# A gated mix of dilated local attention and a 2-D spectral filter: weight blocks prepared once for both parities, odd positions prepared early, folds in other buffers, odd unfolds on GpSimd

## The chip, the cores and the metric

The kernel runs on one core of one Trainium2 chip. The metric is the device time of one execution in microseconds (us). The core has five engines with queues of their own: TensorE (PE, matmuls, with its weight loads shown as PEld), VectorE (DVE), ScalarE (ACT), GpSimd (POOL) and SyncE (SP, which here only issues DMA transfers). A queue is in order: an instruction that waits holds up everything behind it on the same engine.

## The reference, cut to what matters

```python
S, D = 2048, 640                              # positions, channels; everything float32
def _A_ref(x, wqkv, wo):                      # local attention, 32 heads of 20
    W, dil = 8, 2
    qkv = x @ wqkv                            # 640 x 1920, split into q, k, v
    idx = pos[:, None] - (arange(W) * dil)    # a position looks at itself and 7 earlier ones, 2 apart
    logits = where(idx >= 0, einsum("bhsd,bhswd->bhsw", q, k[idx]) * 20 ** -0.5, -1e9)
    o = einsum("bhsw,bhswd->bhsd", softmax(logits), v[idx])
    return o @ wo
def _B_ref(x, w_r, w_i):                      # spectral filter
    return irfft2(rfft2(x) * (w_r + 1j * w_i))
g = sigmoid((x * gate_w).sum(-1, keepdims=True))
return g * _A_ref(x, wqkv, wo) + (1 - g) * _B_ref(x, w_r, w_i)
```

Because the window steps by 2, even positions look only at even ones and odd positions only at odd ones. The two parities are independent in attention.

## The kernel before, in words

**Layout.** A partition holds 16 consecutive positions, j = 0 to 15, so `x` is 128 partitions x 16 positions x 640 channels. Even j belong to parity 0, odd j to parity 1.

**Projection (`load_x`, `load_w`, `qkv`).** TensorE multiplies fp32 numbers as fp32r in three products: each operand is split into a rounded high part (a cast on ScalarE) and a low part (a subtraction on VectorE or GpSimd), and hi x hi, hi x lo and lo x hi are summed. The weights come as four head groups hg = 0 to 3 of five blocks each (128 x 480). For one parity and one hg, `qkv` runs eight positions of fifteen products, copies each result out of PSUM on ScalarE (`ev`) and stores it to DRAM (`qkvd`). Seven PSUM banks (`BP`) rotate among these. Even x (`xe`) and hg 0 are read into the buffers `x0` to `x6` first; odd x (`xo`) comes later, in `x0` to `x7`. Before, all four head groups are run for the even positions (0, 1, 2, 3), then for the odd ones (3, 2, 1, 0). Three of the four weight groups are loaded and split a second time for the odd ones. A split of hg 1 is on VectorE, seven times from a copy in PSUM (`ws`); the other loaded ones are on GpSimd.

**Folds (`fold`, `load_f`, `cols`).** For the transform along the channels, `fold` adds and subtracts mirrored halves of x for two positions at once (q = 0 to 7; six two-input operations on SBUF data, all on VectorE). Folds 0 and 1 stay in SBUF; the other six are stored to DRAM by GpSimd's queue and read back. `cols` multiplies a folded pair by a transform over the partitions (`z`), and ScalarE copies the result into `zg`, which lies where the even x lay. So no `cols` can begin before the last even projection.

**Attention (`attend`).** Sixteen units (parity, h), two per head group. A unit loads k, q, v from DRAM, VectorE multiplies q (copied into the PSUM bank `qbank` by ScalarE) with shifted k (`pr`) and sums over the head's 20 channels (`L`); softmax follows; GpSimd multiplies with v (`pv`) and VectorE sums (`o`), which goes to DRAM (`od`). Some units give the last of their four `pr` to GpSimd. Before, the units are the eight even ones, then the odd ones h = 6, 7, 4, 5, 2, 3 and, interleaved, 0 and 1.

**Spectral stage (`freq`).** Sixteen groups of frequencies in the order 1, 2, 3, 0, 4 to 15. For each: products `u`, `v` over the channels, sum and difference (`ab`), a transform (`xa`, and for the other half `xc`), multiplication by the filter, the transform back (`g`). The filter needs each half also turned by 90 degrees. Groups 0 to 3 get this by a second product (`xb`, `xd`); groups 4 to 15 (`TURN`) by two half-height copies on ScalarE.

**The end (`spatial`, `project_even`, `project_odd`).** `spatial` transforms back over channels and partitions (`oa`, `ob`, `ha`, `hb`). Even rows are unfolded on VectorE (`h`, `ha`, `y`) and added on GpSimd to the projected attention, which was stored before (`yi`). For odd rows the halves are kept (`ho`), and `project_odd` unfolds them in five operations (`ye`, `y`), transposes the attention output (`oTp`, `oT`), multiplies it by `wo` (`woa`, `wob`, 30 products) and adds it to `y`. Four buffers for `y` serve even and then odd rows.

**The order of the work** is planned ahead: a model of the engines (`Plan.cost`, with `LATE` for latencies and `RATE` and `QUEUE` for transfers) gives each instruction a start, and each engine gets its instructions in that order. A hundred random variations are tried on the model. Dependences through buffers are kept, in the order in which the functions are called: a buffer's next owner waits for every access of the owner before. The model lets a VectorE operation with two SBUF inputs wait for GpSimd (`two`, `WAIT`).

All planned instructions have the same line in the profile, 638, so they are told apart by their tiles' names. The lines of the program that the change touches are: the earliest start of loads (297), the planner's constants (476 to 479), the rings of buffers (549 to 556), the order of calls (`work`, 570), `load_w` (656), `load_x` (681), `qkv` (706), `fold` (825), and the tables `WPLACES`, `ODD_POOL`, `FOLD_DVE`, `TURN` (1132 to 1147).

Of the kernel before, what the change touches and what calls it, by code (L numbers as in the profile page):

```python
# [13 lines left out]
F32 = mybir.dt.float32  # L14
# [141 lines left out]
class Plan:  # L156
# [121 lines left out]
    def order(self):  # L278
        ops = self.ops
        for op in ops:  # L280
            op.lat += LATE.get(op.chain, 0.0) * (not op.size or op.chain in ("swap", "f"))
        for op in ops:
            for p in op.preds:
                p.succs.append(op)
        last = {}
        for op in reversed(ops):
            op.tail = max([s.tail + self.lag(op, s) for s in op.succs], default=0.0)
            if op.size:
                op.tail += op.size / RATE
            key = (op.eng, op.chain)  # L290
            if key in last and (op.eng == "PE" or op.chain and op.eng != "ACT"):
                op.tail = max(op.tail, last[key].tail)
            op.tail += op.busy
            last[key] = op
        span = max(op.tail for op in ops)
        for op in ops:
            op.early = max(0.0, span - op.tail - AHEAD) if op.early else 0.0
            op.tail += BIAS.get(op.chain, 0.0)
        rng = np.random.default_rng(SEED)
        self.draws = [rng.exponential(size=len(ops)).tolist() for _ in range(DRAWS)]  # L300
        best = self.turns(TURNS)

        names = {n: i for i, n in enumerate(dict.fromkeys(op.of for op in ops))}
        family = np.array([names[op.of] for op in ops])
        for _ in range(AGAIN):
            move = MOVE * rng.choice([0.3, 1.0, 2.0]) * rng.normal(size=len(names))
            move *= rng.random(len(names)) < rng.choice([0.1, 0.5, 1.0])
            for op, t in zip(ops, (best[1] + move[family]).tolist()):
                op.tail = t
            best = min(best, self.turns(2), key=lambda b: b[0])  # L310
        self.ends = best[0], best[3]
        order = []
        for op, op.start, op.end in best[2]:
            order.append(op)
        return order
# [157 lines left out]
DRAWS, SOONEST, LATER_BY = 3, 2.4, 0.6  # L473
ENGS = ("PE", "DVE", "ACT", "POOL", "SP")
RATE = 380e3
QUEUE = 250e3
LAND = 3.2
LATE = {"w": 1.0, "f": 4.0, "x": 3.5, "swap": 1.5}
AHEAD = 130.0
WAIT = 1.3  # L480
PACE = 1.02
EDGE = {("POOL", "ACT"): 2.0, ("DVE", "ACT"): 1.0}
# [4 lines left out]
def staged(gens, n):  # L487
    for step in range(len(gens) + n - 1):
        for i in range(max(0, step - n + 1), min(step, len(gens) - 1) + 1):
            next(gens[i], None)  # L490
# [14 lines left out]
class Mixer:  # L505
# [17 lines left out]
    def places(self, pp, dr, sb):  # L523
        self.pp, self.sb = pp, sb
        qb = self.pp.tile([128, 512], F32, tag="qbank", name="qbank")
        self.qthird = [qb[:, GC * i : GC * i + GC] for i in range(3)]
        self.qturn = -1
        self.qkv_d = dr.tile([8, 6, ROWS, HC], F32, tag="dram_qkv", name="qkvd")
        self.o_d = [dr.tile([128, 8, D], F32, tag=f"dram_o{i}", name=f"od{i}") for i in range(2)]
        self.f_d = dr.tile([128, 8, 2, D], F32, tag="dram_f", name="fd")  # L530
        self.a_d = dr.tile([128, 8, D], F32, tag="dram_a", name="ad")
        self.ident, self.fc = (self.one(n, 128) for n in ("ident", "fc"))
        self.fct = self.one("fct", 2, 128)
        self.z, self.g, self.ng, self.nng = (self.one(n, NJ) for n in ("z", "g", "ng", "nng"))
        make_identity(self.nc, self.ident)
        self.low = self.one("low", 64)
        self.nc.gpsimd.memset(self.low, -1e9)

        def ring(*tags):
            return Ring(sb, *tags)  # L540

        def n(tag, k):
            return ring(*(f"{tag}{i}" for i in range(k)))


        self.kvr, self.Lr, self.qr, self.prr = n("kv", 6), n("L", 3), n("q", 2), n("pr", 2)
        self.mr, self.sr, self.orr, self.pvr = n("m", 2), n("s", 2), n("o", 2), n("pv", 2)

        self.xr, self.wr, self.evr, self.rawr, self.fr = n("x", 8), ring(*WPLACES), n("ev", 2), n("raw", 5), n("f", 2)
        self.er = ring("e0", "e1")  # L550

        self.zcr, self.vsr, self.mdr, self.mfr, self.wpr = n("raw", 2), ring("raw2"), n("ev", 2), ring("mf"), n("f", 2)
        self.abr, self.Pr, self.s12r, self.Xr = ring("x0", "x1"), ring("x2", "x3"), ring("x4", "x5"), ring("raw3", "raw4")
        self.p1r = ring("x6")

        self.wor, self.war, self.yar = ring("ya", "w7"), n("w", 7), ring("ya")
        self.otr, self.oTr = (ring("w7"), ring("w7", "kv2")), (ring("x7"), ring("x7", "pr0"))
        self.osr, self.hor, self.hyr, self.yer = n("raw", 3), n("x", 4), ring("x4", "x5"), ring("x6")
        self.yr, self.yir = ring("raw3", "raw4", "e0", "ya"), n("f", 2)
        self.banks = {}  # L560
# [9 lines left out]
    def work(self):  # L570
# [12 lines left out]
        S.dma_start(self.fc, ins["t_fc"][:, 0:128])  # L583
        self.zero_rows()
        self.qkv(0, 0)
        self.load_w(None, 1)
        for q in range(8):
            self.fold(q)
        self.qkv(0, 1)
        self.load_w(None, 2)  # L590
        self.qkv(0, 2)
        self.load_w(None, 3)
        for j in range(1, NJ, 2):
            self.load_x(None, self.xr.next(f"xo{j}", 2, 5, 128, dtype=F32R), j)
        self.qkv(0, 3)
        self.zg = self.one("zg", 5, NJ, 128, tag="big")
        for hg in (3, 2, 1, 0):
            self.qkv(1, hg)
            if hg:
                self.load_w(None, hg - 1)  # L600
                for q in {3: (0, 1), 2: (2, 3), 1: (4, 5, 6, 7)}[hg]:
                    self.cols(q)
                    if q < 6:
                        self.load_f(q + 2)
        self.bt, self.gt = self.one("bt", 1288, tag="e0"), self.one("gt", 1288, tag="e1")
        S.dma_start(self.bt[:, 0:1284], ins["t_bt"])
        S.dma_start(self.gt, ins["t_gt"])
        S.dma_start(self.fct.rearrange("p v m -> p (v m)"), ins["t_fc"][:, 128:384])
        self.gates()
        self.load_wo()  # L610
        for h in range(8):
            staged([self.attend(0, h)], 3)
        for h in (6, 7, 4, 5, 2, 3):
            staged([self.attend(1, h)], 3)
        pair = [self.attend(1, h, 2) for h in (0, 1)]
        for _ in range(5):
            for a in pair:
                next(a, None)
# [23 lines left out]

    def zero_rows(self):
        p, d = self.p, self.qkv_d
        zero = self.one("zero", 7 * HC, tag="pv0")[0:32]
        p.pool.memset(zero, 0.0)
        p.pool.dma_start(
            bass.AP(
                tensor=d.tensor,
                offset=d.offset + 2 * ROWS * HC,  # L650
                ap=[[6 * ROWS * HC, 8], [ROWS * HC, 4], [1, 7 * HC]],
            ),
            zero,
        )

    def load_w(self, st, hg):
# [4 lines left out]
        for t in range(5):  # L661
# [5 lines left out]
                p.sp.dma_start(raw, src[t])  # L667
            p.chain = "w" if st is None else ""
            p.act.copy(hi[t], raw)
            if hg == 1 and (t > 2 or 1 in self.xT) or (hg, t, 1 in self.xT) in W_DVE:  # L670
                b = self.ps(BP, f"ws{t}")[:, 0:n]
                p.act.copy(b, raw)
                raw = b
            (p.pool if hg != 1 and st is None and (hg, t, 1 in self.xT) not in W_DVE else p.dve).tensor_sub(lo[t], raw, hi[t].bitcast(F32))
            p.chain = ""

    def load_chunk(self, place, hg, t):
# [3 lines left out]
    def load_x(self, st, pair, j):  # L681
        p = self.p
        hi, lo = self.xT[j] = [pair[:, i].rearrange("p t a -> p (t a)") for i in range(2)]
        raw = (self.rawr.next(f"xt{j}", 640) if st is None else st.pop(0))[:, 0:640]
        self.xraw[j] = raw
        src = self.ins["xT"][j].rearrange("p t a -> p (t a)")
        p.chain = "" if j else "first"
# [15 lines left out]
            (p.pool if st is None else p.dve).tensor_sub(lo, raw, hi.bitcast(F32))  # L703
        p.chain = ""

    def qkv(self, par, hg):
        p, d = self.p, self.qkv_d
        n = 482 if hg == 0 else 480
        u = 4 * par + hg
        for jj in range(8):  # L710
# [17 lines left out]
            if jj % 2:  # L728
# [3 lines left out]
                    ap=[[8 * HC, 128], [ROWS * HC, 6], [1, 2 * HC]],  # L732
                )
                p.act.dma_start(to, ev.rearrange("p i j c -> p i (j c)"))

    def gates(self):
        p = self.p
# [87 lines left out]
    def fold(self, q):  # L825
        p = self.p
        G = p.dve if q in FOLD_DVE else p.pool
        xt = (self.fr if q < 2 else self.xr).next(f"fx{q}", 2, 641)
        p.sp.dma_start(xt, self.ins["x"][:, 2 * q : 2 * q + 2, :])
        e = self.er.next(f"fe{q}", 2, 321)  # L830
        f, o = xt[:, :, 0:640], xt[:, :, 0:321]
        rv = xt[:, :, 640:319:-1]
# [3 lines left out]
        G.tensor_add(f[:, :, 480:640], o[:, :, 1:161], o[:, :, 319:159:-1])  # L836
        G.tensor_add(f[:, :, 0:161], e[:, :, 0:161], e[:, :, 320:159:-1])
        G.tensor_sub(f[:, :, 161:321], e[:, :, 0:160], e[:, :, 320:160:-1])
        if q < 2:
            self.folded[q] = f  # L840
        else:
            p.pool.dma_start(self.f_d[:, q], f)

    def load_f(self, q):
        f = self.folded[q] = self.fr.next(f"f{q}", 2, 641)[:, :, 0:640]
# [283 lines left out]


WA, WB, WC = ("w0", "w1", "w2", "w3", "w4"), ("w5", "w6", "w7", "w0", "w1"), ("w2", "w3", "w4", "e0", "e1")
WPLACES = WA + WB + WC + WB + WC + WB + ("w2", "w3", "w4", "e1", "w5")

WHOLE = tuple((0, t) for t in range(5))
ODD_POOL = ()
XO_DVE = ()
W_DVE = ()
FOLD_DVE = tuple(range(8))

# [2 lines left out]
POOL_PR = {u: (6,) for u in ((0, 3), (0, 4), (0, 5), (0, 7), (1, 0), (1, 1), (1, 3), (1, 4), (1, 5), (1, 7))}  # L1144


TURN = tuple(range(4, 16))


def build(tc, ins, out):  # L1150
# [45 lines left out]
```

## Time and profile before

| | |
|---|---|
| median of 3 runs | 465.52 us (464.35 to 465.58) |
| profiled execution, its own time | 463.47 us |
| its span, first to last instruction | 461.7 us |
| mean granted TensorE clock | 0.996 |
| busy: PE, PEld, DVE, ACT, POOL | 449.5, 393.3, 422.1, 219.4, 319.5 us |
| DMA traffic | 105.90 MB, mean 229 GB/s |
| weight block loads (`raw`) | 25 of 240 KB and 5 of 241 KB |

An engine's busy time is the union of its instructions, and overlapping matmuls are counted once. In a row of groups, "x15 | 25.0, 1560 | 10.5 <-ACT X 10.5" means: fifteen instructions, 25.0 us busy together, 1560 ns one, and 10.5 us in which the engine stood idle before them, released by ScalarE's `X`. A fp32 product shows as two records ("x2").

### The profile page before, as it was taken

The numbers are of one execution on the slowest core, as the hardware profiler recorded it, in microseconds if no ns is written. First come the engines' busy times: TensorE is split into PE (matmuls) and PEld (weight loads), VectorE is DVE, ScalarE is ACT, GpSimd is POOL, SyncE is SP. The second block draws the span as 40 slices with busy tenths as digits, with TensorE's granted clock in tenths as the row PEclk, the third lists the DMA queues.
The fourth block names the chain that finished last, engine by engine and source line by source line (L and its number), as shares of the span: only waits on it lengthen the run. The fifth ranks groups of instructions, "written<-read, shape, count | busy, mean of one in ns | idle before, by whom it ended". The sixth has DMA issues, their size and how long they took to land.

```text
span 461.7 us, 7202 instructions
## 1 busy us (share of the span) xinstructions
PE 449.5 (97%) x2449; PEld 393.3 (85%) x2449; DVE 422.1 (91%) x555; ACT 219.4 (48%) x575; POOL 319.5 (69%) x264
## 2 busy tenths in 40 slices
PE   8899999999999999999999999999999999998997
PEld 4688888888889889899887878879988999987996
DVE  3599979999998999899999999899999999999594
ACT  4432455524326354254457477777665454341110
POOL 1001656999999869879898988477587996964200
PEclk9999999999999999999999999999999999998999
DMA  8999999786777988868887776657643321365832
GB/s 309 395 392 297 371 386 310 260 275 196 249 248 199 324 250 263 267 173 298 294 282 238 216 226 213 236 158 249 192 150 92 89 88 51 128 194 138 267 124 85
DMA packets 71700, 105.90 MB, mean 229 GB/s; under 512 B 20704, under 2 KB 50400, under 8 KB 71664
## 3 DMA queue, kind: packets, MB, share of 16 engines
q1 hardware_dynamic: 40624, 69.90, 46.6%
q10 hardware_dynamic: 30128, 31.55, 21.5%
q0 software_dynamic: 912, 4.00, 2.2%
q8 instruction: 19, 0.31, 0.3%
q14 instruction: 17, 0.14, 0.1%
HBM read 72.59 MB, written 32.84 MB: 228 GB/s over the span
## 4 chain that ended last, share of the span: by engine, by line
PE 83%; DVE 9%; DMA 4%; ACT 2%; issue 2%; SPq 0%; ACTq 0%; DVEq 0%
PE qkv L638 43%; PE woa L638 7%; PE wob L638 6%; PE z L638 4%; PE oa L638 3%; PE ob L638 3%; PE g L638 3%; PE u L638 2%; PE v L638 2%; PE oTp L638 2%; PE xc L638 2%; DMA raw<-in_wqkv 2%; DMA st<-in_xT 1%; PE hb L638 1%; PE ha L638 1%
## 5 line engine op out<-in xcount | busy, mean ns | idle before, releaser
L638 PE MATMUL qkv<-w,xo 128*128 128x480 f32 (+1 forms) x480 | 109.7, 384 | 0.0
L638 PE MATMUL qkv<-w,xe 128*128 128x480 f32 (+1 forms) x465 | 103.4, 382 | 2.1 <-ACT xe L638 1.5
L638 PEld LDWEIGHTS qkv<-w,xe 128*128 128x128 f32 x465 | 87.3, 188 | 18.0 <-ACT xe L638 3.0
L638 PEld LDWEIGHTS qkv<-w,xo 128*128 128x128 f32 x480 | 89.8, 189 | 13.5
L638 ACT COPY ev<-qkv 128x480 f32<-128x480 f32 x64 | 35.3, 559 | 74.5 <-PE qkv L638 69.3
L638 PE MATMUL woa<-wo,oT 128*128 128x320 f32 x240 | 50.6, 321 | 0.0
L638 PE MATMUL wob<-wo,oT 128*128 128x320 f32 x240 | 50.0, 318 | 0.6 <-ACT oT L638 0.6
L638 PEld LDWEIGHTS woa<-wo,oT 128*128 128x128 f32 x240 | 39.4, 192 | 0.5
L638 PEld LDWEIGHTS wob<-wo,oT 128*128 128x128 f32 x240 | 39.0, 190 | 0.9 <-ACT oT L638 0.8
L638 POOL DMA_DIRECT2D fd<-fx x6 | 4.3, 722 | 42.4 <-DVE fx L638 42.4
L638 POOL TENSOR_TENSOR P<-X,wp 128x642 f32<-128x642 f32 x16 | 25.0, 1560 | 10.5 <-ACT X L638 10.5
L638 POOL TENSOR_TENSOR w<-raw,w 128x480 fp32r<-128x480 f32 (+1 forms) x20 | 25.3, 1278 | 8.0 <-ACT w L638 5.3
L638 ACT CAST oT<-oTp 128x384 fp32r<-128x384 f32 (+1 forms) x32 | 13.3, 427 | 31.8 <-PE oTp L638 22.7
L638 PEld LDWEIGHTS g<-mm,s 128*128 128x128 f32 x150 | 22.5, 190 | 6.4 <-ACT zg L638 1.7
L638 PE MATMUL g<-mm,s 128*128 128x128 f32 x150 | 24.9, 278 | 1.4 <-DVE s L638 0.7
L638 PE MATMUL u<-bt,zc 128*128 128x321 f32 (+2 forms) x96 | 23.3, 344 | 0.0
L638 PE MATMUL ob<-gt,zg 128*128 128x161 f32 (+1 forms) x96 | 23.1, 344 | 0.0
L638 PE MATMUL v<-bt,zc 128*128 128x321 f32 (+2 forms) x96 | 22.9, 344 | 0.0
L638 POOL TENSOR_TENSOR yi<-yi,y 128x640 f32<-128x640 f32 x8 | 12.6, 1569 | 14.2 <-DMA yi<-ad 11.4
L638 PE MATMUL oa<-gt,zg 128*128 128x161 f32 (+1 forms) x96 | 22.0, 344 | 0.0
L638 ACT CAST w<-raw 128x480 fp32r<-128x480 f32 (+1 forms) x30 | 17.4, 594 | 7.1 <-PE qkv L638 5.3
L638 DVE TENSOR_TENSOR oT<-oTp,oT 128x384 fp32r<-128x384 f32 (+1 forms) x32 | 15.2, 482 | 3.7 <-ACT oT L638 3.7
(304 smaller groups left out, 1113.6 us busy)
## 6 DMA issues: line engine op xcount, KB each, us to landing
qkvd<-ev ACTq DMA_DIRECT2D x32, 480.0 KB, 4.3
wp<-in_ws SPq DMA_DIRECT2D x16, 642.0 KB, 4.3
raw<-in_wqkv SPq DMA_DIRECT2D x25, 240.0 KB, 6.7
fx<-in_x SPq DMA_DIRECT2D x8, 641.0 KB, 9.0
ot<-od SPq DMA_DIRECT2D x16, 320.0 KB, 3.4
fd<-fx POOLq DMA_DIRECT2D x6, 640.0 KB, 6.0
f<-fd SPq DMA_DIRECT2D x6, 640.0 KB, 5.7
xt<-in_xT SPq DMA_DIRECT2D x8, 320.0 KB, 4.9
```

Source lines behind the costliest of these rows:

```text
L638: p.dve.memset(w, 0.0)
```

## The change

- Each weight group is loaded and split once. The order of projections becomes (even, 0), (odd, 0), (even, 1), (odd, 1), (even, 2), (even, 3), (odd, 2), (odd, 3). Loaded blocks are all split on GpSimd; the copies through PSUM are gone.
- The odd positions are loaded and split right after the even ones, from raw buffers of their own (`xor`).
- The folds use the buffers `pr0`, `pr1`, `pv0`, `pv1`, `f0`, `f1`; folds 6 and 7 stay in SBUF, fold 7 is made by GpSimd, the stores are issued by ScalarE's queue, and the loads have an earliest start in the plan. The zeros for the rows before the first position move from `pv0` to `ya`.
- `cols` are called between the positions of the last two projections, 6 and 7 first.
- The attention units take the order of `UNITS`.
- Odd rows are unfolded on GpSimd.
- Groups 1, 2 and 3 are turned by copies as well.
- The planner's constants for a queue's rate and for the odd positions' lateness change. The raw `wo` blocks keep their buffers, the split ones get others.

```diff
-            op.early = max(0.0, span - op.tail - AHEAD) if op.early else 0.0
+            op.early = max(FOLD * (op.chain == "fold"), span - op.tail - AHEAD) if op.early else 0.0
...
-QUEUE = 250e3
+QUEUE = 330e3
-LATE = {"w": 1.0, "f": 4.0, "x": 3.5, "swap": 1.5}
+LATE = {"w": 1.0, "f": 4.0, "x": 1.0, "swap": 1.5}
+FOLD = 14.0
...
-        self.er = ring("e0", "e1")
+        self.er, self.xor = ring("e0", "e1"), ring("raw0", "raw1", "raw2", "raw3", "raw4", "kv4", "kv5", "ya")
-        self.wor, self.war, self.yar = ring("ya", "w7"), n("w", 7), ring("ya")
+        self.wor, self.war, self.yar = ring("ya", "w7"), ring("w2", "w3", "w4", "w0", "w1", "w5", "w6"), ring("ya")
...
         self.qkv(0, 0)
-        self.load_w(None, 1)
         for q in range(8):
             self.fold(q)
-        self.qkv(0, 1)
-        self.load_w(None, 2)
-        self.qkv(0, 2)
-        self.load_w(None, 3)
         for j in range(1, NJ, 2):
             self.load_x(None, self.xr.next(f"xo{j}", 2, 5, 128, dtype=F32R), j)
-        self.qkv(0, 3)
+        self.qkv(1, 0)
+        for hg in (1, 2, 3):
+            self.load_w(None, hg)
+            self.qkv(0, hg)
+            if hg == 1:
+                self.qkv(1, hg)
         self.zg = self.one("zg", 5, NJ, 128, tag="big")
-        for hg in (3, 2, 1, 0):
-            self.qkv(1, hg)
-            if hg:
-                self.load_w(None, hg - 1)
-                for q in {3: (0, 1), 2: (2, 3), 1: (4, 5, 6, 7)}[hg]:
-                    self.cols(q)
-                    if q < 6:
-                        self.load_f(q + 2)
+        todo = [6, 7, 0, 1, 2, 3, 4, 5]
+
+        def columns(jj):
+            if jj % 2:
+                self.cols(todo.pop(0))
+                if len(todo) > 1:
+                    self.load_f(todo[1])
+
+        self.qkv(1, 2, columns)
+        self.qkv(1, 3, columns)
...
-        for h in range(8):
-            staged([self.attend(0, h)], 3)
-        for h in (6, 7, 4, 5, 2, 3):
-            staged([self.attend(1, h)], 3)
-        pair = [self.attend(1, h, 2) for h in (0, 1)]
+        for u in UNITS[:-2]:
+            staged([self.attend(*u)], 3)
+        pair = [self.attend(*u, 2) for u in UNITS[-2:]]
...
-            if hg == 1 and (t > 2 or 1 in self.xT) or (hg, t, 1 in self.xT) in W_DVE:
-                b = self.ps(BP, f"ws{t}")[:, 0:n]
-                p.act.copy(b, raw)
-                raw = b
-            (p.pool if hg != 1 and st is None and (hg, t, 1 in self.xT) not in W_DVE else p.dve).tensor_sub(lo[t], raw, hi[t].bitcast(F32))
+            (p.dve if st is not None else p.pool).tensor_sub(lo[t], raw, hi[t].bitcast(F32))
...
-        xt = (self.fr if q < 2 else self.xr).next(f"fx{q}", 2, 641)
+        xt = self.one(f"fx{q}", 2, 641, tag=FOLDS[q])
+        p.chain = "fold"
         p.sp.dma_start(xt, self.ins["x"][:, 2 * q : 2 * q + 2, :])
+        p.chain = ""
...
-        if q < 2:
+        if q > 5:
             self.folded[q] = f
         else:
-            p.pool.dma_start(self.f_d[:, q], f)
+            p.act.dma_start(self.f_d[:, q], f)
...
-WPLACES = WA + WB + WC + WB + WC + WB + ("w2", "w3", "w4", "e1", "w5")
+WPLACES = WA + WB + WC + WB
-ODD_POOL = ()
+ODD_POOL = tuple(range(1, 16, 2))
-FOLD_DVE = tuple(range(8))
+FOLD_DVE = tuple(range(7))
-TURN = tuple(range(4, 16))
+TURN = tuple(range(1, 16))
+UNITS = ((0, 0), (0, 1), (1, 0), (1, 1), (0, 2), (0, 3), (0, 4), (0, 5), (0, 6), (0, 7), (1, 2), (1, 3), (1, 4), (1, 5), (1, 6), (1, 7))
+FOLDS = ("pr0", "pr1", "pv0", "pv1", "f0", "f1", "f0", "f1")
```

More of the change, by code (lines that the diff above doesn't have):

```diff
@@ L644, in zero_rows @@
         p, d = self.p, self.qkv_d
-        zero = self.one("zero", 7 * HC, tag="pv0")[0:32]
+        zero = self.one("zero", 7 * HC, tag="ya")[0:32]
         p.pool.memset(zero, 0.0)
@@ L683, in load_x @@
         hi, lo = self.xT[j] = [pair[:, i].rearrange("p t a -> p (t a)") for i in range(2)]
-        raw = (self.rawr.next(f"xt{j}", 640) if st is None else st.pop(0))[:, 0:640]
+        raw = (self.xor.next(f"xt{j}", 640) if st is None else st.pop(0))[:, 0:640]
         self.xraw[j] = raw
@@ L704, in load_x, with qkv @@
         p.chain = ""
-    def qkv(self, par, hg):
+    def qkv(self, par, hg, between=None):
         p, d = self.p, self.qkv_d
@@ L734, in qkv @@
                 p.act.dma_start(to, ev.rearrange("p i j c -> p i (j c)"))
+            if between:
+                between(jj)
     def gates(self):
@@ L1131 @@
 WA, WB, WC = ("w0", "w1", "w2", "w3", "w4"), ("w5", "w6", "w7", "w0", "w1"), ("w2", "w3", "w4", "e0", "e1")
-WPLACES = WA + WB + WC + WB + WC + WB + ("w2", "w3", "w4", "e1", "w5")
+WPLACES = WA + WB + WC + WB
 WHOLE = tuple((0, t) for t in range(5))
-ODD_POOL = ()
+ODD_POOL = tuple(range(1, 16, 2))
 XO_DVE = ()
-W_DVE = ()
-FOLD_DVE = tuple(range(8))
+FOLD_DVE = tuple(range(7))
 ON_ACT = ("vt", "q")
 POOL_PR = {u: (6,) for u in ((0, 3), (0, 4), (0, 5), (0, 7), (1, 0), (1, 1), (1, 3), (1, 4), (1, 5), (1, 7))}
-TURN = tuple(range(4, 16))
+TURN = tuple(range(1, 16))
+UNITS = ((0, 0), (0, 1), (1, 0), (1, 1), (0, 2), (0, 3), (0, 4), (0, 5), (0, 6), (0, 7), (1, 2), (1, 3), (1, 4), (1, 5), (1, 6), (1, 7))
+FOLDS = ("pr0", "pr1", "pv0", "pv1", "f0", "f1", "f0", "f1")
 def build(tc, ins, out):
```

## Prediction

> **What bounds the kernel now.** I read the page's shares first, then the stretches, the chain of waits and TensorE's waits, and for the parts the groups and the timelines of VectorE and GpSimd.
>
> ```profile
> span 461.7 us, 7202 instructions
> ...
> PE 449.5 (97%) x2449; PEld 393.3 (85%) x2449; DVE 422.1 (91%) x555; ACT 219.4 (48%) x575; POOL 319.5 (69%) x264
> ...
> POOL 1001656999999869879898988477587996964200
> ```
>
> TensorE (PE) is busy for 449.5 of 461.7 us, so it has 12.2 us to give back in all; beyond that only fewer matmuls help. VectorE (DVE) at 91% is the second candidate, and GpSimd (POOL) and ScalarE (ACT) have room; POOL's row of 40 slices (11.5 us each, tenths) shows it idle early and full from 80 to 140 us. Where the 12.2 us lie is in the table by stretches (columns: length, then busy time of PE, PEld, DVE, ACT, POOL, then the granted PE clock, DMA share, GB/s):
>
> ```profile
> 0.00:25.00 25.00, 21.02 (x73) 14.57 (x74) 12.52 (x20) 11.16 (x20) 1.99 (x9) 1.00 0.95 357
> 25.00:237.00 212.00, 212.00 (x1050) 185.42 (x1049) 204.19 (x200) 92.75 (x245) 167.25 (x133) 1.00 0.86 278
> 237.00:345.00 108.00, 106.19 (x621) 90.10 (x621) 103.00 (x169) 75.21 (x210) 83.81 (x73) 1.00 0.67 214
> ...
> 410.00:420.00 10.00, 7.55 (x45) 6.40 (x44) 9.41 (x24) 3.58 (x8) 5.39 (x4) 0.90 0.46 140
> 420.00:430.00 10.00, 10.00 (x67) 9.98 (x67) 8.10 (x17) 0.85 (x2) 1.55 (x2) 0.93 0.65 199
> ```
>
> 4.0 us are the opening (25 - 21.02), none lies from 25 to 237, 1.8 us in the spectral stage (108 - 106.19), 2.45 us at 410 to 420 (10 - 7.55), and 3.4 us are the last row's way out (461.7 - 458.33, below). Only there does the granted clock fall, to 0.90 and in the next stretch 0.93. The chain of waits (start, length, what) shows what happens there; its first two rows are used further down:
>
> ```profile
> 5.89 6.87 DMA st<-in_xT
> ...
> 21.33 119.97 PE qkv L638 x547
> ...
> 417.53 0.39 DVE ha L638
> 417.93 0.47 DVE oT L638
> 418.44 0.90 PE oTp L638 x3
> ...
> 434.04 0.55 PE oTp L638 x5
> ...
> 458.33 0.55 DVE y L638
> ```
>
> DVE is the releaser: it is still unfolding even rows while attention's last sums wait, and the next odd block's transpose waits for it. Three transposes then take 0.90 us; five take 0.55 us later, so PE comes out of the hole at about half speed. TensorE's waits name what it stood for longest there:
>
> ```profile
> PE oTp L638 <- DVE oT L638: 1.8, 1, 1.8
> ```
>
> I price the hole at 3.9 us: the 2.45 idle and 1.5 of slow clock (10 x 0.10 + 10 x 0.07 = 1.7 from the clock column, less the share that was idle). From 418.44 PE works without a break to the end. So the end is set by PE's count of matmuls, plus a hole that DVE makes.
>
> **The change, part by part.** The order of all engines is planned anew, which I cannot see; I cost the parts from rows of this trace.
>
> *Turns for groups 1, 2, 3.* They lose the second product of both halves (xb and xd), six products of 321 columns.
>
> ```profile
> 256.75 0.54 PE xb L638 x2
> ...
> L638 ACT COPY xd<-xc 64x321 f32<-64x321 f32 x12 | 4.8, 399 | 3.2 <-DVE p L638 3.0
> ```
>
> PE gets back 6 x 0.54 = 3.25 us. ACT makes, per group, two half copies where it made one whole, and two more, three more in all at 0.40: 3 x 3 x 0.40 = 3.6 us on an engine at 75.21 of 108 us there. A DVE product then waits 0.8 us for ACT instead of 0.54 for PE; other groups' products cover this, as they do for the twelve groups that turn already. Without cover it is (0.8 - 0.54) x 3 = 0.8 us. I take 0, bounds -1.0 (part of the 1.8 us of holes goes) to +1.0.
>
> *Weights once.* Fifteen blocks of 240 KB are neither loaded nor split again, and no block passes through PSUM. DVE loses all ten of its loaded-block splits, and POOL's go from 20 to 15.
>
> ```profile
> L638 DVE TENSOR_TENSOR w<-ws,w 128x480 fp32r<-128x480 f32 x7 | 4.5, 642 | 0.0
> L638 DVE TENSOR_TENSOR w<-raw,w 128x480 fp32r<-128x480 f32 x3 | 1.8, 652 | 0.0
> L638 POOL TENSOR_TENSOR w<-raw,w 128x480 fp32r<-128x480 f32 (+1 forms) x20 | 25.3, 1278 | 8.0 <-ACT w L638 5.3 <-DMA raw<-in_wqkv 2.6
> L638 POOL TENSOR_TENSOR xo<-xt,xo 128x640 fp32r<-128x640 f32 x8 | 12.4, 1580 | 0.0
> ```
>
> DVE: -(4.5 + 1.8) = -6.3 us, half before the first attention and half (3.2) after. ACT loses 15 casts and 7 copies, over 12 us. No PE work goes: the products are the same 945, in another order. The odd positions' splits (12.4 us on POOL) move into the opening.
>
> *Folds.* DVE folds seven instead of eight, POOL the last; stores go from POOL's queue to ACT's.
>
> ```profile
> L638 DVE TENSOR_TENSOR fx<-fx 128x642 f32<-128x642 f32 (+2 forms) x24 | 14.9, 643 | 0.3
> L638 DVE TENSOR_TENSOR fx<-fe 128x322 f32<-128x322 f32 (+1 forms) x16 | 9.4, 610 | 0.2
> L638 DVE TENSOR_TENSOR fe<-fx 128x642 f32<-128x642 f32 x8 | 6.6, 824 | 0.1
> L638 POOL TENSOR_TENSOR P<-X,wp 128x642 f32<-128x642 f32 x16 | 25.0, 1560 | 10.5 <-ACT X L638 10.5
> L638 POOL TENSOR_TENSOR P<-P 128x321 f32<-128x321 f32 x16 | 12.0, 752 | 1.3
> ```
>
> (14.9 + 9.4 + 6.6) / 8 = 3.9 us leave DVE; on POOL the same six operations are 2 x 1.56 + 4 x 0.75 = 6.1 us. ACT's six store issues each wait for a fold, with the copies out of PSUM and attention's q copies queued behind. I take 0: seven banks at 15 x 0.22 = 3.3 us of PE work each cover some 23 us of such a wait for PE; without cover a late fold costs its lateness.
>
> *The opening, where the sum is least sure.* POOL now runs 8 odd splits (12.4), five splits of block set 1 (5 x 1.28 = 6.4) and a fold (6.1), 24.9 us, beside DVE's folds; today it is idle there (the second to fourth slices of its row: 0, 0, 1). Where the two overlap today, they block each other:
>
> ```profile
> 24.61 1.76 DVE L638 TENSOR_TENSOR fx<-fx 128x642 f32<-128x642 f32 x3
> ...
> 45.95 0.89 DVE L638 TENSOR_TENSOR fx<-fe 128x322 f32<-128x322 f32 x2
> ...
> 48.42 2.83 DVE L638 TENSOR_TENSOR fx<-fe 128x322 f32<-128x322 f32 x2
> 51.17 2.77 DVE L638 TENSOR_TENSOR fx<-fx 128x642 f32<-128x642 f32 x3
> ...
> 54.79 2.88 DVE L638 TENSOR_TENSOR pr0a<-kt0a,qbank 128x1280 f32<-128x1280 f32 x2
> ...
> 47.87 4.46 POOL L638 TENSOR_TENSOR w<-raw,w 128x480 fp32r<-128x480 f32 x3
> ```
>
> The pair took 2.83 instead of 0.89, the three 2.77 instead of 1.76: 2.95 us lost to 4.46 us of POOL work, a share of 0.66. DVE's first attention product starts at 54.79. Without that loss, the five splits (3.2) and a fold (3.9) it would start at 44.7; with a share s of 24.9 us lost, at 44.7 + 24.9 s. s is bounded by 0 and 1; I take 0.4, below 0.66 because part of POOL's work will meet an idle DVE (12.52 of the first 25 us busy). That gives 54.7: no gain and no loss here. DVE then has 3.2 us less of splits, and no odd unfolds among its attention:
>
> ```profile
> 386.24 1.51 DVE L638 TENSOR_TENSOR ye<-ho 128x322 f32<-128x322 f32 x1
> ...
> 396.42 1.48 DVE L638 TENSOR_TENSOR ye<-ho 128x160 f32<-128x160 f32 x1
> ```
>
> Those two took 3.0 us ahead of the hole. So DVE reaches the hole 3.2 + 3.0 + 0.1 = 6.3 us earlier, and PE 3.25 us earlier. The hole needs 3.25 + 3.9 = 7.1 us to close fully; 6.3 leaves 0.8, so I take 3.0 of 3.9 (bounds 0 and 3.9).
>
> The Trainium skill states a harder case, in "SBUF — State Buffer", Who interferes with whom: a VectorE instruction with two SBUF inputs and a GpSimd instruction that reads SBUF exclude each other for the whole instruction. By it s could reach 1, and the sum would be that of rival B at its far end; the trace's 0.66 lies below it.
>
> PE's own opening: odd products start near 39 us (the even ones follow the load that ends at 5.89 + 6.87 = 12.8, and 120 of them at 119.97 / 547 = 0.22 take 26 us). The odd loads (8 x 320 KB) take the place of set 1's and 2's (10 x 240 KB), so traffic up to then stays alike (357 GB/s over the first 25 us). I take 0. Bounds: -1.5 (the wait below, ACT held by a weight load, goes) to +1.5 (the same wait again for an odd block).
>
> ```profile
> PE qkv L638 <- ACT xe L638: 1.5, 1, 1.5
> ```
>
> *Odd unfolds on POOL.*
>
> ```profile
> L638 DVE TENSOR_TENSOR ye<-ho 128x160 f32<-128x160 f32 (+1 forms) x24 | 10.3, 466 | 0.2
> L638 DVE TENSOR_TENSOR y<-ye 128x321 f32<-128x321 f32 (+1 forms) x16 | 8.6, 569 | 0.1
> 435.25 1.57 POOL L638 TENSOR_TENSOR yi<-yi,y 128x640 f32<-128x640 f32 x1 [1.48 <-DMA yi<-ad]
> ...
> L638 POOL TENSOR_TENSOR yi<-yi,y 128x640 f32<-128x640 f32 x8 | 12.6, 1569 | 14.2 <-DMA yi<-ad 11.4
> ```
>
> DVE loses 18.9 us, but 15.9 of them in the tail, where PE sets the pace: nothing. POOL pays, by the 0.75 row, 3 x 0.75 + 2 x 0.38 = 3.0 us a position, 24 us in all. PE needs (458.33 - 418.44) / 8 = 5.0 us a position, so POOL keeps up if it starts in time: 0, priced in rival C if not.
>
> *Sum.* The profiled execution took 463.47 us (span 461.7 and 1.8 around it). 463.47 - 3.25 - 3.0 = 457.2. The median of the runs, 465.52, lies 2.05 above that execution; with it the forecast is **459.3 us**.
>
> **The rivals.**
>
> *A, everything closes.* The hole goes (3.9), with the 1.5 in the opening and 1.0 of the spectral holes: 465.52 - 3.25 - 6.4 = 455.9. For it: POOL, full at 80 to 140 us today, is rid of the splits it does there. Against: each needs the new order to be right at once.
>
> *B, POOL blocks DVE in the opening.* At s = 0.66, attention starts at 61.1, the 6.2 us won later are eaten, and DVE reaches the hole when it does today: PE merely waits longer there, 465.5 (rival "no change"). Beyond 0.66 it is slower: at 0.8 attention starts at 64.6 and the end moves by 9.8 - 6.2 = +3.6 to 469.1; at 1, by 14.8 - 6.2 = +8.6 to 474.1. For it: the two rows at 48 and 51 us. Against: POOL has about 25 us for this work until the folds end, so it is not back to back, as it was at 48 us.
>
> *C, POOL is late in the tail.* Its order is fixed, and it stood 11.4 us for the loads of even rows there. If the odd unfolds stand behind the last even addition (435.25 + 1.57 = 436.8), the last is done at 436.8 + 24 = 460.8, then 0.55 and 3.4 us follow: 464.8, +3.1, 468.6. It decides from a start later than 458.33 - 24 = 434.3. Against: two or more odd rows have free buffers before that.
>
> *D, what is said to be removed stays in another form* (a longer wait for the one preparation): the shared end again, 465.5; counted with "no change".
>
> **How the numbers follow.** Forecast 0.60, own range 457 to 462.5; A 0.14; no change 0.10; B beyond 0.66 0.08 (0.02 of it at its far end); C 0.08. A difference under 0.3% (1.4 us) can't be told from none. Faster: 0.60 + 0.14 = 0.74; same 0.10; slower 0.16. The range goes from 455 (A with a little more) to 466.5, taking in "no change" and leaving out most of B and C.
>
> **What would show it.** Right: xb and xd left with group 0 alone; PE's wait on DVE's oT near 410 to 420 under 1 us, its clock 1.00 there; first attention product at 50 to 58 us; no PE hole from 25 to 237. Wrong: fold pairs of over 2 us through the opening and attention later than 61 us (B); PE waiting near the end on banks that wait for y from POOL (C); a PE wait on odd blocks at 38 to 60 us.

## The result, and the profile after

The median after is 457.37 us (457.05 to 457.69), beside 465.55 us (464.35 to 466.13) before, a ratio of 0.9827 with a 95% interval of 0.9807 to 0.9848. The forecast was 459.3, with an own range of 457 to 462.5. The profiled execution took 457.05 us. The page's first lines after (span; busy time; POOL's and the granted clock's rows of 40 slices, 11.4 us each):

```profile
span 455.2 us, 7081 instructions
...
PE 444.1 (98%) x2437; PEld 390.1 (86%) x2437; DVE 408.0 (90%) x499; ACT 211.0 (46%) x562; POOL 344.2 (76%) x299
...
POOL 1394056799999878998949894958597688888794
PEclk9999999999999999999999999999999999999999
```

PE lost 5.4 us of work (449.5 to 444.1) and 1.1 us of idle time (12.2 to 11.1); together they are the 6.5 us of span. The table by stretches after has the columns of the one before:

```profile
0.00:25.00 25.00, 23.12 (x84) 17.29 (x85) 13.15 (x18) 15.33 (x28) 8.06 (x13) 1.00 0.95 362
25.00:237.00 212.00, 211.58 (x1046) 184.64 (x1045) 207.57 (x189) 75.84 (x211) 164.67 (x127) 1.00 0.80 263
237.00:345.00 108.00, 103.65 (x618) 88.68 (x617) 102.19 (x166) 81.76 (x228) 83.51 (x71) 1.00 0.65 213
...
410.00:420.00 10.00, 9.00 (x63) 8.45 (x63) 9.76 (x21) 2.70 (x6) 8.67 (x9) 1.00 0.58 178
420.00:430.00 10.00, 10.00 (x72) 9.98 (x72) 4.86 (x9) 1.51 (x4) 7.18 (x10) 1.00 0.84 268
```

Idle time of PE, length less busy time:

| stretch | before | after | difference | forecast |
|---|---|---|---|---|
| opening, 0 to 25 | 3.98 | 1.88 | -2.10 | 0 |
| 25 to 345, spectral stage included | 1.81 | 4.77 | +2.96 | 0 |
| the hole, 410 to 420 | 2.45 | 1.00 | -1.45 | with the clock -3.0 |
| the rest | 3.97 | 3.47 | -0.50 | 0 |

The granted clock is 1.00 in every stretch, so the 1.5 us that the prediction gave to slow work after the hole are gone too. What is left of the 5.4 us of work are the turns (3.25) and 0.7 that I can't assign. TensorE's waits after:

```profile
PE oTp L639 <- DVE oT L639: 1.6, 4, 0.6
PE xa L639 <- DVE ab L639: 1.3, 1, 1.3
...
PE xa L639 <- ACT xd L639: 0.6, 1, 0.6
PE g L639 <- ACT zg L639: 0.6, 1, 0.6
PE v L639 <- ACT zc L639: 0.4, 1, 0.4
```

The one wait of 1.8 us on `oT` has become four of at most 0.6. The opening's wait on `xe` is gone. New are waits at the start of the spectral stage: on `zc` (the last columns now come directly before it) and on `ab`. The groups of `xb`, in the view of that tile, and of the unfolds on POOL:

```profile
L639 PE MATMUL xb<-ab,tbfirst x4: 431/434/436, 259.2 to 260.0; 128*128 128x321 f32 x4
...
L639 POOL TENSOR_TENSOR ye<-ho 128x160 f32<-128x160 f32 (+1 forms) x24 | 12.9, 565 | 0.6
...
L639 POOL TENSOR_TENSOR y<-ye 128x321 f32<-128x321 f32 (+1 forms) x16 | 11.7, 753 | 0.6
```

Only group 0 (`tbfirst`) still has `xb`. The odd unfolds are 24.6 us of POOL, as priced. VectorE's timeline in the opening, and GpSimd's:

```profile
22.82 5.68 DVE L639 TENSOR_TENSOR fx<-fx 128x642 f32<-128x642 f32 x3
28.54 3.54 DVE L639 TENSOR_TENSOR fx<-fe 128x322 f32<-128x322 f32 x2
...
34.24 1.76 DVE L639 TENSOR_TENSOR fx<-fx 128x642 f32<-128x642 f32 x3
36.03 0.90 DVE L639 TENSOR_TENSOR fx<-fe 128x322 f32<-128x322 f32 x2
...
39.30 4.61 DVE L639 TENSOR_TENSOR fx<-fx 128x642 f32<-128x642 f32 x3
...
53.04 1.48 DVE L639 TENSOR_TENSOR pr0a<-kt0a,qbank 128x1280 f32<-128x1280 f32 x1
```

```profile
20.53 12.98 POOL L639 TENSOR_TENSOR xo<-xt,xo 128x640 fp32r<-128x640 f32 x7 [1.49 <-ACT xo L639]
38.69 4.87 POOL L639 TENSOR_TENSOR w<-raw,w 128x480 fp32r<-128x480 f32 x3 [5.17 <-ACT w L639]
```

A triple of folds takes 5.68 or 4.61 us beside POOL's subtractions, and 1.76 in the gap between them (33.5 to 38.7). Attention starts at 53.04.

### The profile page after: what moved, and what is told of

Its sections match the earlier page's. It is cut to its first block, busy times and chain, and to the rows that moved or that the text cites. A ratio compares the mean times of both kernels' runs of the same rounds, so it can differ in the third digit from the quotient of the medians.

```text
span 455.2 us, 7081 instructions
## 1 busy us (share of the span) xinstructions
PE 444.1 (98%) x2437; PEld 390.1 (86%) x2437; DVE 408.0 (90%) x499; ACT 211.0 (46%) x562; POOL 344.2 (76%) x299
## 4 chain that ended last, share of the span: by engine, by line
DVE 44%; PE 25%; DMA 15%; issue 7%; POOL 4%; ACT 3%; ACTq 1%; SPq 0%; DVEq 0%; POOLq 0%
DMA qkvd<-ev 7%; PE woa L639 6%; PE wob L639 5%; PE g L639 2%; PE oa L639 2%; DVE xd L639 2%; PE ob L639 2%; PE u L639 2%; PE v L639 2%; DVE fx L639 1%; POOL pv0b L639 1%; DMA xt<-in_xT 1%; DMA od<-o1b 1%; DMA st<-in_w 1%; PE oTp L639 1%
## 5 line engine op out<-in xcount | busy, mean ns | idle before, releaser
L639 PE MATMUL qkv<-w,xo 128*128 128x480 f32 (+1 forms) x480 | 115.8, 388 | 0.0
L639 POOL TENSOR_TENSOR w<-raw,w 128x480 fp32r<-128x480 f32 x15 | 19.5, 1328 | 26.2 <-ACT w L639 25.7
L639 POOL TENSOR_TENSOR P<-X,wp 128x642 f32<-128x642 f32 x16 | 24.9, 1558 | 17.3 <-ACT X L639 17.2
L639 POOL TENSOR_TENSOR xo<-xt,xo 128x640 fp32r<-128x640 f32 x8 | 14.6, 1857 | 16.4 <-ACT xo L639 16.4
L639 PE MATMUL oa<-gt,zg 128*128 128x161 f32 (+1 forms) x96 | 23.0, 344 | 0.0
L639 PEld LDWEIGHTS z<-fc,f 128*128 128x128 f32 x120 | 19.1, 191 | 1.5
L639 DVE TENSOR_TENSOR fx<-fx 128x642 f32<-128x642 f32 (+2 forms) x21 | 19.7, 975 | 0.3
```

The costliest lines, as they stand in the source:

```text
L639: p.dve.memset(w, 0.0)
```

## The experiments

They were run in three groups, each beside the kernel before on the same chip. Its median there was 463.36, 463.79 and 463.13 us, some 2 us below the 465.55 of the first comparison, so a ratio belongs to its own group. The kernel after itself was not run in these groups. The clock that an execution was granted explains much of the spread. In the third group the kernel before took 461.0 to 463.3 us at 1.000, 463.1 to 465.2 at 0.996 and 465.3 to 466.6 at 0.993, while the four executions of the kernel after were all at 1.000.

| kernel | group | median, us | ratio to before, 95% |
|---|---|---|---|
| after, groups 1 to 3 turned by products | 1 | 461.32 | 0.9958, 0.9936 to 0.9979 |
| after, odd unfolds on VectorE | 1 | 462.04 | 0.9933, 0.9902 to 0.9963 |
| after, seed 3 | 1 | 460.72 | 0.9927, 0.9904 to 0.9950 |
| before, seed 3 | 1 | 457.91 | 0.9870, 0.9847 to 0.9894 |
| after, columns earlier | 2 | 460.97 | 0.9931, 0.9905 to 0.9957 |
| after, columns earlier, seed 3 | 2 | 457.92 | 0.9858, 0.9825 to 0.9891 |
| after, seed 4 | 2 | 456.08 | 0.9827, 0.9799 to 0.9855 |
| before, seed 4 | 2 | 457.07 | 0.9845, 0.9817 to 0.9872 |
| after, six products twice | 3 | 459.98 | 0.9935, 0.9906 to 0.9964 |
| before, six products twice | 3 | 466.61 | 1.0060, 1.0036 to 1.0083 |
| after, odd low parts left out | 3 | 456.65 | 0.9848, 0.9818 to 0.9879 |
| before, seed 4, groups 1 to 3 turned by copies | 3 | 462.56 | 0.9988, 0.9964 to 1.0011 |

### One part undone, planned anew

```diff
-TURN = tuple(range(1, 16))
+TURN = tuple(range(4, 16))
```

> The changed kernel with groups 1 to 3 turned by a second product again (six products of 0.54 us more on TensorE, nine half copies less on ScalarE). Theory, TensorE's count sets the end: 457.4 + 3.25 = 460.6 us, with TensorE busy 3.3 us more. Rival, VectorE sets the end and the six products only filled holes: 457.4 us, and TensorE's holes of 4.35 us at 237 to 345 us shrink to about 1.8, since the copies on ScalarE made them.

```diff
-ODD_POOL = tuple(range(1, 16, 2))
+ODD_POOL = ()
```

> The changed kernel with the odd rows unfolded on VectorE again. Theory, TensorE's count sets the end and VectorE only makes the hole near 410 us: VectorE is some 3 us later there, so the hole comes back by up to 3 us, 458 to 460 us. Rival, VectorE's total sets the end: it gets 18.9 us more and the end moves by a good part of that, 465 us or more. Second rival, GpSimd was the slower place for the unfolds (the last odd rows wait for it): faster than 457.4 us.

Measured were 461.32 and 462.04 us. Neither is a clean answer, because each edit lets the planner make another order. With the turns undone PE's work rises by 3.5 us (444.1 to 447.6), but the opening also has a new wait. With the unfolds on VectorE a new hole opens at the start of the spectral stage. The wait of the first, and the stretch and the waits of the second:

```profile
PE qkv L639 <- DMA st<-in_xT: 3.6, 1, 3.6
```

```profile
200.00:260.00 60.00, 56.09 (x309) 48.51 (x308) 58.26 (x61) 33.37 (x93) 48.74 (x42) 0.97 0.88 291
...
PE v L639 <- ACT zc L639: 3.8, 1, 3.8
PE oTp L639 <- DVE oT L639: 1.2, 1, 1.2
```

The second kernel's executions fall apart by the granted clock: 457.1 to 458.5 us at 1.000, 461.6 to 463.3 at 0.992 to 0.996. At the full clock it is as fast as the kernel after (457.05 to 457.69), with 19 us more on VectorE (427.3 against 408.0) and 1.2 us on `oT` against 1.6. So in that order the place of the odd unfolds shows no cost of its own; the two kernels were not timed on one chip. The extra 4 us of the others go with a lower clock, which in the profiled one falls to 0.97 in the stretch of the new hole.

### Another order, the same program

`SEED` picks the planner's random variations and changes nothing else.

```diff
-TURNS, AGAIN, MOVE, SEED = 6, 100, 2.0, 2
+TURNS, AGAIN, MOVE, SEED = 6, 100, 2.0, 3
```

> The changed kernel, planned with another random seed; no work is changed, only the order. Theory, the gain comes from work removed and moved: within 2 us of 457.4. Rival, the gain is luck of one order: 460 to 466 us.

> The kernel before, planned with another random seed. Theory: within 2 us of 465.5, with a hole of TensorE near 410 us again. Rival, the order before was an unlucky one: 458 to 462 us.

The signs are reversed: before 457.91, after 460.72. The unchanged program, in another order, gains 1.3% where the whole change gained 1.7%; its longest wait on `oT` is 0.6 us, without one edit to VectorE's work. The changed program in this order has a hole of 4.5 us, and ScalarE's timeline shows what made it:

```profile
237.81 0.30 ACT L639 COPY qbank<-q5b 128x160 f32<-128x160 f32 x1 [4.08 <-DMA q5b<-qkvd]
...
239.40 0.86 ACT L639 COPY zg<-z 128x512 f32<-128x512 f32 x2 [0.45 <-ACT ev L639]
```

ScalarE stood 4.08 us for one load of q, and the last column copies were queued behind it. This is the exposure that the change's order of calls makes: the last columns have no projection behind them that could cover a late copy.

### The columns earlier

The columns are called at every position of `qkv(1, 2)`, none at `qkv(1, 3)`, so that a whole head group of products stands behind them; once with seed 2 and once with seed 3.

```diff
-            if jj % 2:
+            if True:
...
-        self.qkv(1, 3, columns)
+        self.qkv(1, 3)
```

> The changed kernel with all eight column transforms called between the positions of the second last projection, none in the last, so that the last projection's 25 us of products can stand beside the start of the spectral stage, as they could before the change. No work is added or taken away. With seed 3 the changed kernel stood 4.5 us there for ScalarE's zc, and its clock was low after it. Theory, the late columns are what the change pays: TensorE's holes from 237 to 345 us shrink from 4.35 to 2.5 us or less, 455 to 457 us. Rival, those holes come from ScalarE's turns: they stay, 457.4 us.

> The same edit with seed 3. Theory: the wait of 4.5 us for zc is gone and the clock stays at 1.00, so 4 to 6 us less than with the late columns: 455 to 457 us against 460.7. Rival, any order has such a hole somewhere: 459 us or more.

The wait on `zc` goes in both, but the time does not follow simply. With seed 2 it is 460.97, with a new wait of 1.9 us on a weight split in the middle of the projections. With seed 3 it is 457.92, 2.8 less than with the late columns, though 2.4 us of waits on folded x (`z` on `f`) have come instead. TensorE's idle time from 237 to 345 us fell from 4.35 to 3.36 us with seed 2, short of the 2.5 expected, and from 5.08 to 1.69 us with seed 3. The exposure is real and can be removed; a new order costs or wins as much on the way.

### A third order, and the turns in it

```diff
-TURNS, AGAIN, MOVE, SEED = 6, 100, 2.0, 2
+TURNS, AGAIN, MOVE, SEED = 6, 100, 2.0, 4
```

> The changed kernel with a third seed. Theory, its work is 3.3 us less on TensorE and its holes vary by order: 455 to 461 us. Rival, seed 2 was a lucky one and seed 3 the rule: 460 us or more.

> The kernel before with a third seed. Theory, the same sum with 3.3 us more on TensorE: 458 to 464 us, by its holes. Rival, seed 2 was the unlucky one and seed 3 the rule: 458 us or less.

456.08 after, 457.07 before. The first is the lowest median of the study, at a ratio that equals the kernel after's in its own comparison, so it isn't shown to beat it. Over the three orders the ratios are 1, 0.9870 and 0.9845 for the program before and 0.9827, 0.9927 and 0.9827 for the program after. Their means differ by 0.0045, about 2 us, with single orders up to 4.4 us from their mean.

Then the turns alone, in the program before with seed 4:

```diff
-TURN = tuple(range(4, 16))
+TURN = tuple(range(1, 16))
```

> The kernel before with seed 4 and one part of the change alone, the turns of groups 1 to 3. Theory, where no hole waits for VectorE the six products count: 3.3 us less than before with seed 4, near 453.8 us, give or take 2 us of the new order; this would be faster than both kernels. Rival, a new order takes it back: 456 us or more.

462.56, 5.5 us more than with seed 4 alone, though six products are gone. Its waits name what the new order brought:

```profile
PE qkv L638 <- ACT xe L638: 1.9, 1, 1.9
PE woa L638 <- DVE oT L638: 1.7, 1, 1.7
```

These are the opening's wait and the hole of the kernel before, come back in another program. A saving of 3.25 us was less than a new order took.

### The order kept

These three kernels keep the planned order and change only what is issued. The six products in question are issued twice (before: `xb`, `xd` of groups 1 to 3; after, where these are gone: `xa`, `xc`).

```diff
                 exec(*op.call)
+                if op.name == "matmul" and op.of.split("_")[0] in ('xa1', 'xa2', 'xa3', 'xc1', 'xc2', 'xc3'):
+                    exec(*op.call)
```

> The changed kernel with its order kept, but the products xa and xc of groups 1 to 3 issued twice: six products of 0.54 us more on TensorE, at the place where the turns took six away. Theory, TensorE's count sets the end here: +3.25 us, 460.6. Rival, the holes of 4.35 us at 237 to 345 us take them up because VectorE sets the pace there: 457.4 to 458.5.

> The kernel before with its order kept, but the products xb and xd of groups 1 to 3 issued twice: 3.25 us more on TensorE. Theory, the hole near 410 us is made by VectorE at a fixed time, so TensorE only comes to it later: the hole of 2.45 us fills, the clock stays up (1.5 us), and the time stays within 1.5 us of the kernel before on the same chip. Rival, TensorE's count sets the end here too: +3.25 us.

After: 459.98 against 457.37, +2.6, though on another chip; executions at the clock of 1.000 have 458.3 to 460.3. Before: 466.61 against 463.13, +3.5; at like clocks about +2.3 to +2.5 (464.0 and 465.1 against a median of 462.3 at 1.000; 466.6 against 464.1 at 0.996). So six products cost 2.1 to 3.5 us where the order stays, most of the 3.25.

The second run refutes a step. I held VectorE to arrive at the hole at a time of its own, so that a PE later by 3.25 us would have waited that much less. The stretch of the hole in the kernel before, then the same in this kernel with TensorE's wait there:

```profile
400.00:440.00 40.00, 37.55 (x243) 35.31 (x242) 33.88 (x72) 11.58 (x27) 20.07 (x15) 0.96 0.62 194
```

```profile
400.00:440.00 40.00, 37.54 (x241) 35.32 (x240) 33.86 (x69) 11.57 (x27) 22.92 (x17) 0.96 0.57 181
...
PE oTp L640 <- DVE oT L640: 1.8, 1, 1.8
```

The hole is there unchanged, 2.46 us against 2.45. VectorE's timeline shows where it became late, first in the kernel before, then here:

```profile
242.48 0.25 DVE L638 RECIPROCAL g<-g 128x16 f32<-128x16 f32 x1
...
271.51 0.49 DVE L638 TENSOR_TENSOR p<-xc,wp 128x321 f32<-128x321 f32 x1 [0.31 <-ACT xd L638]
...
417.84 0.55 DVE L638 TENSOR_TENSOR oT<-oTp,oT 128x384 fp32r<-128x384 f32 x1
```

```profile
242.48 0.25 DVE L640 RECIPROCAL g<-g 128x16 f32<-128x16 f32 x1
...
253.62 0.49 DVE L640 TENSOR_TENSOR p<-xc,wp 128x321 f32<-128x321 f32 x1 [0.47 <-PE xc L640]
...
274.35 0.49 DVE L640 TENSOR_TENSOR p<-xc,wp 128x321 f32<-128x321 f32 x1 [0.93 <-ACT xd L640]
...
420.68 0.55 DVE L640 TENSOR_TENSOR oT<-oTp,oT 128x384 fp32r<-128x384 f32 x1
```

The first row starts at 242.48 us in both. Then come the groups with the doubled products. VectorE works on what PE delivers there and waits for it: among others 0.47 us for `xc`, and 0.93 instead of 0.31 us for the copy of `xd`. At 274.35 it is 2.84 us late, and at the hole still 2.84 (420.68 against 417.84), like PE, whose waiting transposes start at 421.28 instead of 418.44.

In the third kernel GpSimd writes zeros as the odd positions' low parts, so the products that need them add nothing; the subtractions (12.98 us and more, above) are left out.

```diff
+                if op.eng == "POOL" and op.name == "tensor_sub" and op.of.startswith("xo"):
+                    self.pool.real.memset(op.call[1]["a"][0].bitcast(F32), 0.0)
+                    continue
                 exec(*op.call)
```

> The changed kernel with its order kept, but GpSimd writes zeros as the low parts of the odd positions (memset, which reads nothing) in place of the eight subtractions: the odd positions lose their low parts. Theory, GpSimd's reading of SBUF blocks VectorE's folds: the folds from 21.6 us on lose about 7 us less, the first attention product starts where its data arrive, 49 to 51 us instead of 53.0; the end stays within 1 us of 457.4, since TensorE's work sets it. Rival, the folds are slow for another reason: they stay, attention starts at 53. Second rival, VectorE's start sets the end: 2 to 3 us less.

Its timelines of VectorE and GpSimd:

```profile
22.16 1.75 DVE L642 TENSOR_TENSOR fx<-fx 128x642 f32<-128x642 f32 x3
23.95 0.90 DVE L642 TENSOR_TENSOR fx<-fe 128x322 f32<-128x322 f32 x2
...
39.93 2.83 DVE L642 TENSOR_TENSOR fx<-fe 128x322 f32<-128x322 f32 x2
...
43.60 0.90 DVE L642 TENSOR_TENSOR fx<-fe 128x322 f32<-128x322 f32 x2
49.43 1.49 DVE L642 TENSOR_TENSOR pr0a<-kt0a,qbank 128x1280 f32<-128x1280 f32 x1 [4.93 <-ACT qbank L642]
```

```profile
38.16 4.25 POOL L642 TENSOR_TENSOR w<-raw,w 128x480 fp32r<-128x480 f32 x3 [20.57 <-ACT w L642]
```

The first triple takes 1.75 us where it took 5.68, and the folds are still slow where a weight split remains beside them (2.83 at 39.93). They end at 44.5 instead of 53.0. Attention starts 3.6 us earlier, held by the load of q, but the span is only 0.4 us shorter (454.8) and the median 0.7 (456.65).

Even these 0.4 us are not attention's. VectorE's lead of 3.6 us is down to 0.4 at its next such product, which waits for q again (56.95 against 57.33 us). PE was ahead before attention began, by 1.9 us at its first products with the split `w` and `xe` (9.04 against 10.96 us), because its very first products were faster in this execution (see the last section). Near 62 us, at the next weight splits, it waited 0.75 us and kept 0.5 of that lead.

## Why the prediction was right, and where it was not

**PE's count sets the end: right.** The six products left with groups 1 to 3, and issuing six such products more cost 2.1 to 3.5 us where only they were changed; the term was 3.25.

**The hole closes by 3.0: right in size, wrong in reason.** The idle time fell by 1.45, and with the clock at 1.00 the 1.5 priced for slow work went too, 2.95 in all. The step "DVE reaches the hole 6.3 us earlier, and PE 3.25 us earlier. The hole needs 7.1 us" failed: VectorE has no time of its own there. Where PE is late by six products in the spectral stage, VectorE, which takes its operands from PE's products in that stage, is late with it, by 2.84 us each, and the hole stays as it was. Nor was less work on VectorE needed: seed 3 and seed 4 close the hole of the kernel before with all odd unfolds still on it: PE stands at most 0.6 us at a time there. The hole belonged to one order. That after's order has none, and the lighter VectorE's part in that, the runs don't separate. Two readings of rows were off besides, with little effect on the sum: a third odd unfold (0.32 us at 391.43) also stood ahead of the hole, and 0.30 against 0.11 us for a transpose is not half speed; the price of the slow work came from the clock column.

**PE's opening 0: wrong,** by 2.1 us, beyond the bound of -1.5. The bound named the wait on `xe`, and that went. I kept it at 0 for want of the new order; other orders of the changed program lose it again (3.6 us on `in_xT` with the turns undone). Nor is the change shown to be its cause: with seeds 3 and 4 the program before has no wait on `xe` either.

**The spectral stage 0: wrong,** by +2.96 us, beyond the bound of +1.0. I priced only the turns' latency, and the new wait on a turned copy (`xd`) is 0.6 us, inside the bound. I overlooked that the columns, moved to the last projections, put `zc` and `ab` directly behind the last column copies, with no projection left for PE to do meanwhile. The first `ab` then stood behind two attention sums of VectorE:

```profile
238.34 2.82 DVE L639 TENSOR_REDUCE L5a<-pr5a 128x64 f32<-128x1280 f32 x2
241.07 0.89 DVE L639 TENSOR_TENSOR ab<-u,vs 128x321 f32<-128x321 f32 x2
```

These two misses have opposite signs. With 1.2 us of small gains (0.5 of idle time, 0.7 of work) they cancel. That was luck, and only so the sum of 457.2 met the profiled 457.05. It also kept rival A (455.9) away: its opening came, its spectral part came with the other sign.

**The median's 2.05 above the profile: wrong.** That offset was the kernel before's own: its executions vary with the clock granted (as the third group shows), those of the kernel after did not (median 457.37 against the profiled 457.05). So the forecast of 459.3 was high by 1.9.

**s = 0.4: too low, and without effect.** With and without the odd subtractions the folds took 31.45 us (21.59 to 53.04) and 23.2 us (21.30 to 44.50): 8.25 us lost to the 12 us of subtractions that ran beside them from 21.59 on (to 33.51), a share of 0.69, close to the 0.66 read before. The Trainium skill's exclusive lock ("SBUF — State Buffer", Who interferes with whom) agrees in kind, not in the full share of 1 that I took from it as a far end. Attention still came at 53.04 (54.7 forecast), by two errors that partly cancel. Only 16.8 of the 24.9 us of GpSimd's work fell there, as two of the five splits and fold 7 came after 61 us; at the higher share the loss was some 11.1 us (8.25, and 2.85 in the triple at 39.30) where 10.0 were forecast. And without any loss the folds would have ended near 42 instead of 44.7 us (an estimate from these rows). A wait for q, which the prediction did not have, holds attention until 49.43 even where the folds end at 44.5. The start of attention did not set the end: 3.6 us earlier came with 0.4 to 0.7 us at the end, and in the profiled execution PE's faster first products account for it. The far side of rival B, a later start, was not tried.

**Odd unfolds on POOL 0, rival C: right.** GpSimd was in time; its first and last unfolding additions:

```profile
417.55 1.47 POOL L639 TENSOR_TENSOR y<-ye 128x321 f32<-128x321 f32 x2
...
447.35 1.47 POOL L639 TENSOR_TENSOR y<-ye 128x321 f32<-128x321 f32 x2
```

It began at 417.55, well before the 434.3 from which C decides, and PE had no idle time from 420 to 430.

What stays open: how much of the 8 us the change is worth apart from the order it happened to get. Its turns are worth 2 to 3.5; over three orders of each program the mean difference was about 2 us, and three orders that spread by 5 and 7 us don't make that figure firm. The weights prepared once, the new places of the folds and the order of the attention units were not tried apart.

## What to carry to other kernels

Where a planner makes the order, time the old and the new program under several orders before a gain is credited to an edit: here the order alone moved one program by about 7 us and the other by 4.6, beside 8 for the whole change. To price one part, keep the order and issue that part twice, or leave it out. And of a stall between two engines ask first whether the late engine has a time of its own or is carried along by the one that waits for it.

## What the runs showed of the hardware

- One kernel's executions fall into groups by the granted clock, 1.000, 0.996 and 0.993, at 462.3, 464.1 and 465.3 us in the middle for the kernel before in the third group. The kernel before has two idle stretches close together ahead of its slow spell (the figures in brackets):

```profile
415.83 0.56 PE L638 MATMUL wob<-wo,oT 128*128 128x320 f32 x2 [0.57 <-ACT oT L638]
...
418.44 0.90 PE L638 MATMUL oTp<-ident,ot 128*128 128x128 f32 x3 [1.76 <-DVE oT L638]
```

  So 2.3 us of idle time in two pieces went ahead of a slow spell in the profiled execution; executions at a mean clock of 1.000 had no such spell.
- The same 2449 records of products kept PE busy for 449.5, 447.6 and 443.8 us in the three orders of the kernel before. Part of it lies in the first fp32 products, which are slow in some executions. They took 1.95 and 4.35 us in the kernel before, and 1.05 and 3.40 us with seed 4:

```profile
4.79 1.95 PE L638 MATMUL qkv<-st 128*128 128x482 f32 x2 [0.80 <-DMA st<-in_xT]
6.53 4.35 PE L638 MATMUL qkv<-st,st 128*128 128x482 f32 x8
```

```profile
6.20 1.05 PE L638 MATMUL qkv<-st 128*128 128x482 f32 x2 [2.21 <-DMA st<-in_xT]
7.08 3.40 PE L638 MATMUL qkv<-st,st 128*128 128x482 f32 x8
```

  With seed 4 they began 1.4 us later and ended even a little earlier (10.48 against 10.88 us). Neither the order nor the start decides this: the kernel after and its variants with six products twice and without odd low parts have one order, and there the first two took 1.95, 1.05 and 1.05 us from starts at 4.80, 4.63 and 4.67 us. A single record takes 1010 ns in the slow case and 567 ns in the fast one. The Trainium skill ("TensorE: Matmul & The Clock Gate", Part 1) gives a window of about 3.4 us that runs freely, so that the same kernel shows more or fewer slow products at its start from run to run. The traces agree: their clock records begin at 9.67 us in the kernel after and at 3.99 and 4.36 us in the other two, and the slow products all begin before that. So two single profiled executions can differ by some 2 us in the opening without any edit.
